# Upper and lower f16 halves of the keys written in place by ScalarE and VectorE, and value loads of two batches called earlier

## The chip, the cores and the metric

The kernel runs on one core of a Trainium2 chip. A core has five engines that run side by side, each in its own order: TensorE (PE, matrix products), VectorE (DVE), ScalarE (ACT), GpSimd (POOL) and SyncE (SP, which here only issues DMAs). 16 DMA engines move data between HBM and the on-chip memory SBUF, which has 128 partitions. The metric is the device time of one execution in microseconds (us).

## The reference

Three layers follow one another: attention over 4 batches, 8 heads, 576 positions and 64 dimensions; a layer of eight experts with one expert for each of 2304 tokens; a layer with squared rectification.

```python
scores = scale * np.matmul(q, k.transpose(0, 1, 3, 2))
psi_rel = np.log1p(np.abs(pos[:, None] - pos[None, :]))
x = (psi_rel / psi_i)[..., None]
bias = np.maximum(x @ w1 + b1, 0.0) @ w2
scores = scores + bias.transpose(2, 0, 1)[None]
attn = softmax(scores)
x = np.matmul(attn, v)                       # tokens x 512
expert_idx = np.argmax(xn @ en.T / tau, axis=1)
out[mask] = gate_w[mask, None] * (np.maximum(x[mask] @ w1[e], 0) @ w2[e])
r = np.maximum(out @ w_in, 0.0)
return (r * r) @ w_out
```

The change lies in the attention only: in how the keys k are brought into the form in which the score products read them.

## The kernel before, in words

Attention fills the time to about 390 us, the experts run to about 640 us, the last layer to the end. The attention works on 72 units (128 positions of one batch and one pair of heads), each in two half steps, one for each head. In a half step (the loop over `hs` in `attention`) every engine gets a fixed set of instructions in a fixed order: TensorE computes scores (`emit_qk`, L498), transposes the exponentials of an earlier half step (`emit_T`, L531) and multiplies with the values (`emit_pv`, L556); VectorE adds the position bias and takes the extreme (`emit_max`, L509); ScalarE takes the exponential (`emit_exp`, L522); one of the two copies the transposed values (L207 on ScalarE, L209 on VectorE). The schedule is written by hand. Twelve half steps with negative numbers come first, in which `first(i)` computes the first bias groups.

Beside the units run background tasks, each a generator that does one piece at a time and then gives way (`yield E_`). `bg(hs, f, ...)` starts one at a half step, `at(hs, f, ...)` calls a function once. `room` lets a task wait while the load counted for ScalarE ("A") or VectorE ("D") is above a limit, until a due half step; `take` and `give` count buffers. Engine queues run in order: an instruction that waits holds everything emitted behind it on its engine, and a DMA that waits for its data holds SyncE's queue.

The scores need f16 precision twice over: a key is split in an upper half (f16 of 8k) and a lower half (8k minus the upper, in f16). The tile `kst[b]` has 128 partitions: for the first head of a pair the upper half lies in partitions 0 to 63 and the lower half in 64 to 127, for the second head the other way round, so that one product of 128 rows sums both. `kst[0]` holds batches 0 and 1, `kst[2]` batches 2 and 3, with four head pairs (`pr`) in each.

Before, each of the eight (batch pair, head pair) blocks is loaded (`k_load`, L227) into a `wr` buffer of 128 partitions with two batches of 576 keys. `k_hi` (L232) writes the upper half of all 128 partitions with one ScalarE instruction into a `wh` buffer, `k_lo` (L237) the lower half with one VectorE instruction, and `k_move` (L246, L247) brings them with four DMAs of 64 partitions each to their rows of `kst`. For batches 0 and 1 `first` does this (`FK` names the steps), for batches 2 and 3 the task `prep_k`, started at half steps 6 to 9. There are two `wr` and two `wh` buffers. The task `presplit` (32 times from half step 14, one each 2.6 half steps) uses the same buffers for the second expert weights: load (L465), three steps of wait, product on GpSimd (L471), two steps, difference on VectorE (L475), store (L479). The values of batches 1, 2, 3 are loaded (`load_v`, L307) at half steps 0, 16 and 20.

Of the kernel before, what the change touches and what calls it, by code (L numbers as in the profile page):

```python
# [8 lines left out]
F16 = mybir.dt.float16  # L9
U32 = mybir.dt.uint32  # L10
I32 = mybir.dt.int32
AF = mybir.ActivationFunctionType
ALU = mybir.AluOpType
# [4 lines left out]
B, H, S, D = 4, 8, 576, 64  # L18
# [5 lines left out]
P = 128  # L24
# [11 lines left out]
QS, KS = -2.0, 8.0  # L36
# [47 lines left out]
def body(ctx: ExitStack, tc: tile.TileContext, q, k, v, wsm, emb, tau, mw1, mw2, win, wout, cst_d, lsk_d, ids_d, out):  # L84
    nc = tc.nc
    win, wout = win.bitcast(U32), wout.bitcast(U32)
    PE, ACT, DVE, POOL, SP = nc.tensor, nc.scalar, nc.vector, nc.gpsimd, nc.sync
# [39 lines left out]
    def attention(actx, bctx, cctx, smp, mid, early, G):  # L127
# [10 lines left out]
        whp = bp("a_wh", 2)  # L138
# [45 lines left out]
        def take(r, n=1):  # L184
            while free[r] < n:
                yield E_
            free[r] -= n

        def later():
            if now[0] > 8:  # L190
                yield E_

        def give(r, n=1):
            free[r] += n

        def room(e, n, due=1000):
            while load[e] > 0 and load[e] + n > LIM and now[0] < due:
                yield E_
# [12 lines left out]
        def A(n, extra=0.09):  # L211
            load["A"] += n * 0.000833 + extra

        def V(n, extra=0.07):
            load["D"] += n * 0.00104 + extra
# [11 lines left out]
            SP.dma_start(out=t, in_=k[b:b + 2, pr].rearrange("b p s -> p b s"))  # L227
            return t

        def k_hi(t):  # L230
            kh = whp.tile([P, 2, 2, S], F16, name="wh")
            ACT.activation(kh[:, 0], t, AF.Copy, scale=KS)  # L232
            A(2 * S)
            return kh

        def k_lo(t, kh):
            DVE.scalar_tensor_tensor(out=kh[:, 1], in0=t, scalar=KS, in1=kh[:, 0], op0=ALU.mult, op1=ALU.subtract)  # L237
            V(2 * S)

        def k_move(b, pr, kh, eng=SP):  # L240
            if b not in kst:
                kst[b] = (G["kv"].rearrange("p (r h b s) -> p r h b s", r=NP, h=2, b=2) if b == 0 else
                          kvp.tile([P, NP, 2, 2, S], F16, name="kst", bufs=1))
            for h2 in range(2):
                r, o = slice(64 * h2, 64 * h2 + 64), slice(64 - 64 * h2, 128 - 64 * h2)
                eng.dma_start(out=kst[b][r, pr, h2], in_=kh[r, 0])  # L246
                eng.dma_start(out=kst[b][o, pr, h2], in_=kh[r, 1])  # L247
            kready.add((b, pr))

        def prep_k(b, pr, wait):  # L250
            due = 8 * b + 4 * pr
            yield from take("wr")
            t = k_load(b, pr)
            for _ in range(wait):
                yield E_
            yield from take("wh")
            yield from room("A", 1.1, due - 8)
            kh = k_hi(t)
            yield E_
            yield from room("D", 1.3, due - 7)  # L260
            k_lo(t, kh)
            give("wr")
            yield from later()
            k_move(b, pr, kh)
            give("wh")


        def q_load(c, b):
# [79 lines left out]
        def first(i):  # L348
# [41 lines left out]
            for j in range(4):  # L390
                x = "k%d" % j
                if i == FK[j]:
                    f_in[x] = f_in[x], k_hi(f_in[x])
                if i == FK[j] + 1:
                    k_lo(*f_in[x])
                    if j < 2:
                        f_in["k%d" % (j + 2)] = k_load(0, j + 2)
                    else:
                        give("wr")
                if i == FK[j] + 2:  # L400
                    k_move(0, j, f_in[x][1])
                    if j > 1:
                        give("wh")

        for r in ("wr", "wh", "qraw"):
            free[r] = 0
        FQ = 1, 8
        FK = 2, 5, 9, 9
# [51 lines left out]
        def presplit(i):  # L460
            e, j = divmod(i, 4)
            s = W2S
            yield from take("wr")
            wr = wrp.tile([P, 2, S], F32, name="wr").rearrange("p b s -> p (b s)")[:, :1024]
            SP.dma_start(out=wr, in_=mw2[e, j])  # L465
            for _ in range(3):
                yield E_
            yield from take("wh")
            wf = whp.tile([P, 2, 2, S], F16, name="wh").rearrange("p a b s -> p (a b s)")[:, :2048]
            wh = wf.rearrange("p (a n) -> p a n", a=2)  # L470
            POOL.tensor_tensor(out=wh[:, 0], in0=wr, in1=w2s_c.to_broadcast([P, 1024]), op=ALU.mult)  # L471
            for _ in range(2):
                yield E_
            yield from room("D", 1.2)
            DVE.scalar_tensor_tensor(out=wh[:, 1], in0=wr, scalar=s, in1=wh[:, 0], op0=ALU.mult, op1=ALU.subtract)  # L475
            V(1024)
            yield E_
            give("wr")
            SP.dma_start(out=wsc2[i * P:(i + 1) * P, :], in_=wf)  # L479
            yield E_  # L480
            yield E_
            give("wh")
# [287 lines left out]
        def at(hs, f, *a):  # L770
            side.setdefault(max(HS0, hs), []).append((f, a, None))
# [9 lines left out]
        for pr in range(NP):  # L781
            bg(int(6 + 1 * pr), prep_k, 2, pr, 3)
        for b in range(1, 4):
            at((HS0 + 2, HS0 + 12, 16, 20)[b], load_v, b)
        at(26, lambda: SP.dma_start(out=id_d.rearrange("(p n) c -> p (n c)", p=P), in_=ids_d.bitcast(U32)))
        bg(-4, consts)
        bl = list(bfirst)
# [797 lines left out]
```

## Time and profile before

| what | us |
|---|---|
| three runs | 1024.21, 1023.83, 1018.97 |
| their median | 1023.83 |
| profiled execution, its own time | 1020.09 |
| its span in the profile | 1018.3 |
| TensorE busy in the span | 946.7 (93%) |
| VectorE busy | 662.0 (65%) |
| ScalarE busy | 540.9 (53%) |
| GpSimd busy | 499.1 (49%) |

TensorE's granted clock over the span is 0.978 of full speed. A busy share is a mean over stages with different limits, and TensorE's matmuls overlap in the pipeline, so 93% does not mean that it works at its peak. The profile names for each instruction the idle time before it and what ended it; these waits are what tells a transfer that holds an engine from one that is hidden.

### The profile page before, as it was taken

How to read it: one execution, taken by the hardware profiler on the slowest of the kernel's cores; microseconds unless marked ns; L12 is line 12 of the kernel's file. 1: busy time of each engine (PE TensorE's matmuls, PEld its weight loads, DVE VectorE, ACT ScalarE, POOL GpSimd, SP SyncE). 2: the span in 40 equal slices, each digit the busy share in tenths (PEclk: the TensorE clock that was granted, in tenths of full speed). 3: DMA queues.
4: the chain of work that ended last, by engine and by line, in shares of the span. 5: the costliest groups of instructions: out<-in, count | busy, mean ns of one | idle time of the engine just before them, and what ended most of it. 6: DMA issues, size and time to landing. Idle time of an engine off the chain costs nothing. (4 is left out here: it accounts for less than half of the span.)

```text
span 1018.3 us, 24810 instructions
## 1 busy us (share of the span) xinstructions
PE 946.7 (93%) x9725; PEld 747.8 (73%) x9725; DVE 662.0 (65%) x1229; ACT 540.9 (53%) x1000; POOL 499.1 (49%) x415
## 2 busy tenths in 40 slices
PE   8687988999899889999999899999999999999995
PEld 4355766677577767776666667688888888888884
DVE  6655899888997874677776767245446455545441
ACT  5666776767777683467565555255423333233330
POOL 1212536446534353366548797275454554645631
PEclk9789999999999999999999999999999999999998
DMA  9998885898779434599899484462011111111000
GB/s 296 318 254 264 305 279 179 267 268 286 226 234 330 163 126 176 213 338 334 325 361 340 146 291 151 153 258 53 22 54 43 32 52 43 32 53 22 22 12 32
DMA packets 78843, 187.17 MB, mean 184 GB/s; under 512 B 26648, under 2 KB 26776, under 8 KB 76128
## 3 DMA queue, kind: packets, MB, share of 16 engines
q1 hardware_dynamic: 72656, 169.98, 49.5%
q0 software_dynamic: 6064, 15.54, 4.4%
q8 instruction: 78, 1.28, 0.5%
q14 instruction: 45, 0.37, 0.1%
HBM read 171.65 MB, written 51.73 MB: 219 GB/s over the span
## 5 line engine op out<-in xcount | busy, mean ns | idle before, releaser
L1436 POOL TENSOR_TENSOR gf<-gf 128x256 f32<-128x256 f32 x144 | 166.0, 1172 | 131.0 <-DVE gf L1433 108.8
L1420 PE MATMUL pf<-big,wih 128*128 128x256 f16 x1728 | 196.0, 273 | 1.5 <-PEq L1374 1.5
L1420 PEld LDWEIGHTS <-wih 128*128 128x128 f16 x1728 | 169.0, 98 | 21.6 <-issue 2.0
L1458 PEld LDWEIGHTS <-g 128*128 128x128 f16 x1512 | 147.4, 98 | 18.7 <-issue 1.0
L1426 ACT ACTIVATE gf<-pf 128x512 f32<-128x512 f32 x72 | 42.5, 597 | 193.3 <-PE pf L1420 140.3
L1220 PE MATMUL ph<-x,w1b 128*128 128x128 f16 x2112 | 127.5, 220 | 7.9 <-DVEq L1024 3.0
L1220 PEld LDWEIGHTS <-w1b 128*128 128x128 f16 x2112 | 122.0, 99 | 13.1 <-DVEq L1024 3.5
L471 POOL TENSOR_TENSOR wh<-wr,w2s_c 128x1024 f16<-128x1024 f32 x32 | 62.2, 1943 | 135.9 <-DMA wr<-in_mw_dram 65.0
L1235 PE MATMUL py<-vt,h 128*128 128x512 f16 x528 | 119.4, 383 | 3.8 <-DMA vt<-wsc 3.8
L1444 DVE TENSOR_TENSOR g<-gf,g 128x1792 f16<-128x1792 f32 x36 | 85.5, 2374 | 50.1 <-ACT g L1443 50.1
L522 ACT ACTIVATE pr<-ssb,mn 128x576 f32<-128x576 f32 x144 | 111.7, 776 | 10.3 <-DVE mn L509 10.3
L509 DVE CUSTOM_DVE_ANT_0 ssb<-ps_s,bias 128x576 f32<-128x576 f32 x144 | 107.4, 749 | 3.1 <-DMA bias<-bias_d 2.2
L1433 DVE TENSOR_TENSOR gf<-gf 128x1024 f32<-128x1024 f32 x28 | 34.3, 1226 | 113.6 <-ACT gf L1426 113.6
L498 PE MATMUL ps_s<-kst,qd 128*128 128x288 f16 (+1 forms) x640 | 96.6, 292 | 11.7 <-DVE mn L509 9.2
L1235 PEld LDWEIGHTS <-h 128*128 128x128 f16 x528 | 51.3, 99 | 63.0 <-issue 7.0
L531 PE MATMUL ps_t<-cst,pr 128*128 128x128 f32 x576 | 92.1, 283 | 2.5 <-DVE pl L607 1.3
L531 PEld LDWEIGHTS ps_t<-cst,pr 128*128 128x128 f32 x576 | 64.9, 144 | 25.7 <-issue 20.8
L556 PE MATMUL pv<-pt,vt 128*64 128x128 f32 (+1 forms) x1280 | 83.6, 274 | 0.0
L498 PEld LDWEIGHTS <-qd 128*128 128x128 f16 (+1 forms) x640 | 56.2, 101 | 26.6 <-issue 16.4
L556 PEld LDWEIGHTS pv<-pt,vt 128*64 128x64 f32 x1280 | 65.5, 140 | 12.5 <-issue 11.4
L1226 DVE SCALAR_TENSOR_TENSOR h<-ph,h 128x512 f16<-128x512 f32 x44 | 30.3, 690 | 49.9 <-ACT h L1225 35.0
L1443 ACT CAST g<-gf 128x1792 f16<-128x1792 f32 x36 | 60.3, 1676 | 4.4 <-POOL gf L1436 4.4
(194 smaller groups left out, 1571.9 us busy)
## 6 DMA issues: line engine op xcount, KB each, us to landing
vt<-wsc SPq DMA_DIRECT2D x88, 512.0 KB
wr<-in_mw_dram SPq DMA_DIRECT2D x76, 512.0 KB
kst<-in_mw_dram SPq DMA_DIRECT2D x44, 512.0 KB
wsc<-wh SPq DMA_DIRECT2D x32, 512.0 KB
bias<-bias_d SPq DMA_DIRECT2D x16, 576.0 KB
bias_d<-rt SPq DMA_DIRECT2D x28, 295.5 KB
qd<-qh SPq DMA_DIRECT2D x64, 128.0 KB
wr<-in_win_dram SPq DMA_DIRECT2D x8, 1024.0 KB
```

The source lines that it names most:

```text
L471: POOL.tensor_tensor(out=wh[:, 0], in0=wr, in1=w2s_c.to_broadcast([P, 1024]), op=ALU.mult)
L498: PE.matmul(s[r, hf, :288], lhsT=qd[:, h2, i, pr, r], rhs=kst[x - x % 2][:, pr, h2, x % 2, js], start=(i == 0), stop=(i == 1))
L509: DVE.tensor_tensor_reduce(out=ss.rearrange("p (a j) -> p a j", a=2), in0=s[:, :, :288], in1=btile[bkey[u]][:, h2].rearrange("p (a j) -> p ...
L522: ACT.activation(pr_sb[k_ // 2][:, h2], ssb.pop(k_), AF.Exp, bias=mns.pop(k_), scale=-1.0, accum_out=sums[c, b][:, h:h + 1])
L531: PE.transpose(pt_ps[k_][:, jc * P:(jc + 1) * P], src[:, j0:j0 + P], eye)
L556: PE.matmul(pv[o, cs], lhsT=vb[:, 2 * jc + h2, d] if jc < 4 else vb[o, 8, d], rhs=a[h2][:, jc, cs] if jc < 4 else e[o, cs], start=(jc == 4 ...
L1220: PE.matmul(p_[:, f4, :], lhsT=w[:, a, kc, f * P:(f + 1) * P], rhs=x2[:, b, kc, :], start=(i == 0), stop=(i == 11))
L1235: PE.matmul(p_, lhsT=h2[:, a, fc, :], rhs=wb2[fc // 2][:, b, fc % 2, :], start=(i == 0), stop=(i == 23))
L1420: PE.matmul(p_[:, h], lhsT=wih[:, a, kc, f * P:(f + 1) * P], rhs=y2[:, b, kc, :], start=(i == 0), stop=(i == 11))
L1436: POOL.tensor_tensor(out=g[:, d], in0=g[:, x], in1=g[:, y], op=op)
L1444: DVE.tensor_tensor(out=gt[:, 1, :, c:c + 2, :], in0=g[:, 1:8], in1=gt[:, 0, :, c:c + 2, :], op=ALU.subtract)
L1458: PE.matmul(ps, lhsT=gt[:, a, s, c, :], rhs=woh[:, c, b, w, :], start=(i == 0 and first), stop=(i == 23 and end), skip_group_check=True)
```

## The change

The upper half is written by ScalarE straight into `kst`, in two instructions of 64 partitions, one for each head of the pair. The lower half is written by VectorE straight into the other 64 partitions of `kst`, again in two instructions; they read the upper half from `kst`. `k_move` and its 32 DMAs go, and the keys no longer use a `wh` buffer. `presplit`, the other user of these buffers, waits two steps instead of three between its load and GpSimd's product, and has both `wh` buffers from the start. The values of batches 2 and 3 are loaded at half steps 14 and 17 instead of 16 and 20.

```diff
-        def k_hi(t):
-            kh = whp.tile([P, 2, 2, S], F16, name="wh")
-            ACT.activation(kh[:, 0], t, AF.Copy, scale=KS)
-            A(2 * S)
-            return kh
-        def k_lo(t, kh):
-            DVE.scalar_tensor_tensor(out=kh[:, 1], in0=t, scalar=KS, in1=kh[:, 0], op0=ALU.mult, op1=ALU.subtract)
-            V(2 * S)
-        def k_move(b, pr, kh, eng=SP):
+        def k_hi(b, pr, t, h2):
             if b not in kst:
                 kst[b] = (G["kv"].rearrange("p (r h b s) -> p r h b s", r=NP, h=2, b=2) if b == 0 else
                           kvp.tile([P, NP, 2, 2, S], F16, name="kst", bufs=1))
-            for h2 in range(2):
-                r, o = slice(64 * h2, 64 * h2 + 64), slice(64 - 64 * h2, 128 - 64 * h2)
-                eng.dma_start(out=kst[b][r, pr, h2], in_=kh[r, 0])
-                eng.dma_start(out=kst[b][o, pr, h2], in_=kh[r, 1])
-            kready.add((b, pr))
+            r = slice(64 * h2, 64 * h2 + 64)
+            ACT.activation(kst[b][r, pr, h2], t[r], AF.Copy, scale=KS)
+            A(2 * S)
+        def k_lo(b, pr, t, h2):
+            r, o = slice(64 * h2, 64 * h2 + 64), slice(64 - 64 * h2, 128 - 64 * h2)
+            DVE.scalar_tensor_tensor(out=kst[b][o, pr, h2], in0=t[r], scalar=KS, in1=kst[b][r, pr, h2],
+                                     op0=ALU.mult, op1=ALU.subtract)
+            V(2 * S)
+            if h2:
+                kready.add((b, pr))
...
-            yield from take("wh")
-            yield from room("A", 1.1, due - 8)
-            kh = k_hi(t)
-            yield E_
-            yield from room("D", 1.3, due - 7)
-            k_lo(t, kh)
+            for h2 in range(2):
+                yield from room("A", 1.1, due - 8)
+                k_hi(b, pr, t, h2)
+            yield E_
+            for h2 in range(2):
+                yield from room("D", 1.3, due - 7)
+                k_lo(b, pr, t, h2)
             give("wr")
-            yield from later()
-            k_move(b, pr, kh)
-            give("wh")
...
                 if i == FK[j]:
-                    f_in[x] = f_in[x], k_hi(f_in[x])
+                    for h2 in range(2):
+                        k_hi(0, j, f_in[x], h2)
                 if i == FK[j] + 1:
-                    k_lo(*f_in[x])
+                    for h2 in range(2):
+                        k_lo(0, j, f_in[x], h2)
...
-                if i == FK[j] + 2:
-                    k_move(0, j, f_in[x][1])
-                    if j > 1:
-                        give("wh")
-        for r in ("wr", "wh", "qraw"):
+        for r in ("wr", "qraw"):
             free[r] = 0
...
-            for _ in range(3):
+            for _ in range(2):
                 yield E_
             yield from take("wh")
...
-            at((HS0 + 2, HS0 + 12, 16, 20)[b], load_v, b)
+            at((HS0 + 2, HS0 + 12, 14, 17)[b], load_v, b)
```

## Rows read from the trace of the kernel before

**Rows 1.** Stretches: length, busy time by engine (instructions), granted clock, DMA share, GB/s

```profile
core 0: us, PE busy (x) PEld busy (x) DVE busy (x) ACT busy (x) POOL busy (x), PEclk, DMA share, GB/s
48.00:50.00 2.00, 2.00 (x23) 1.71 (x19) 1.74 (x5) 1.76 (x6) 0.00 (x0) 1.00 1.05 395
54.00:70.00 16.00, 13.48 (x132) 9.05 (x132) 13.68 (x32) 13.68 (x33) 1.92 (x2) 0.99 0.84 195
64.00:66.00 2.00, 2.00 (x26) 1.41 (x24) 1.86 (x5) 0.51 (x1) 0.00 (x0) 1.00 1.05 205
...
72.00:74.00 2.00, 2.00 (x17) 1.26 (x16) 0.00 (x0) 0.00 (x0) 0.00 (x0) 0.50 1.07 268
...
76.00:92.00 16.00, 15.52 (x156) 12.34 (x152) 12.79 (x35) 13.03 (x32) 1.90 (x1) 0.98 0.84 240
100.00:340.00 240.00, 224.99 (x2509) 165.88 (x2507) 212.51 (x529) 173.67 (x445) 112.26 (x63) 0.99 0.80 260
```

**Rows 2.** TensorE in order of time: start, duration, instruction, idle time before and releaser

```profile
42.79 0.66 PE L531 MATMUL ps_t<-cst,pr 128*128 128x128 f32 x4
...
68.54 0.33 PE L536 MATMUL pv<-cst,pr 128*128 128x128 f32 x1 [1.66 <-ACT big L207]
68.71 0.60 PE L531 MATMUL ps_t<-cst,pr 128*128 128x128 f32 x4
71.36 1.12 PE L498 MATMUL ps_s<-kst,qd 128*128 128x288 f16 x4 [2.06 <-DMA kst<-wh]
...
76.22 0.77 PE L531 MATMUL ps_t<-cst,pr 128*128 128x128 f32 x4
...
91.14 0.60 PE L531 MATMUL ps_t<-cst,pr 128*128 128x128 f32 x4
...
98.67 0.69 PE L556 MATMUL pv<-pte,vt 64*64 64x128 f32 x4 [6.43 <-DMA vt<-in_v_dram]
...
101.19 1.12 PE L531 MATMUL ps_t<-cst,pr 128*128 128x128 f32 x4
```

**Rows 3.** Instructions on buffer wh: count, duration in ns (min/median/max), first and last start

```profile
L475 DVE SCALAR_TENSOR_TENSOR wh<-wr,wh x32: 1209/1222/2862, 92.2 to 332.9; 128x1024 f16<-128x1024 f32 x32
...
L246 SPq DMA_DIRECT2D kst<-wh x16: 462/570/1133, 16.8 to 87.5; - x16
L247 SPq DMA_DIRECT2D kst<-wh x16: 461/600/1632, 17.4 to 88.1; - x16
L232 ACT ACTIVATE wh<-wr x8: 1152/1162/1187, 10.4 to 80.3; 128x1152 f16<-128x1152 f32 x8
L237 DVE SCALAR_TENSOR_TENSOR wh<-wr,wh x8: 1346/1356/1360, 13.4 to 82.9; 128x1152 f16<-128x1152 f32 x8
```

**Rows 4.** VectorE in order of time, same columns as TensorE's

```profile
32.42 1.36 DVE L237 SCALAR_TENSOR_TENSOR wh<-wr,wh 128x1152 f16<-128x1152 f32 x1 [1.75 <-ACT wh L232]
...
37.56 0.76 DVE L509 CUSTOM_DVE_ANT_0 ssb<-ps_s,bias 128x576 f32<-128x576 f32 x1 [2.24 <-DMA bias<-bias_d]
...
60.94 1.35 DVE L237 SCALAR_TENSOR_TENSOR wh<-wr,wh 128x1152 f16<-128x1152 f32 x1
62.22 0.74 DVE L509 CUSTOM_DVE_ANT_0 ssb<-ps_s,bias 128x576 f32<-128x576 f32 x1
```

**Rows 5.** ScalarE in order of time

```profile
65.49 1.17 ACT L232 ACTIVATE wh<-wr 128x1152 f16<-128x1152 f32 x1 [1.85 <-DMA wr<-in_k_dram]
```

**Rows 6.** SyncE in order of time

```profile
81.47 0.47 SPq L246 DMA_DIRECT2D kst<-wh  x1
...
88.13 0.59 SPq L247 DMA_DIRECT2D kst<-wh  x1
...
89.40 0.61 SPq L307 DMA_DIRECT2D vt<-in_v_dram  x1
```

**Rows 7.** GpSimd's L471 and VectorE's L475 in time; then L471's waits (us, times)

```profile
123.01 1.90 POOL L471 TENSOR_TENSOR wh<-wr,w2s_c 128x1024 f16<-128x1024 f32 x1 [4.09 <-DMA wr<-in_mw_dram]
126.11 2.45 DVE L475 SCALAR_TENSOR_TENSOR wh<-wr,wh 128x1024 f16<-128x1024 f32 x1
...
317.62 1.90 POOL L471 TENSOR_TENSOR wh<-wr,w2s_c 128x1024 f16<-128x1024 f32 x1 [2.17 <-DMA wr<-in_mw_dram]
320.61 1.22 DVE L475 SCALAR_TENSOR_TENSOR wh<-wr,wh 128x1024 f16<-128x1024 f32 x1
...
  DMA wr<-in_mw_dram: 65.0, 20
...
  DVE wh L475: 4.7, 2
```

## The prediction, before the change was run

> **What bounds the kernel now.** I read four views in this order. First the stretches by 2 us, to see where TensorE stands still while the DMA engines do not: from 48 to 50 us the DMA share is 1.05 at 395 GB/s and TensorE works, from 64 to 66 the share is the same but only 205 GB/s go through, and from 72 to 74 TensorE runs at a granted clock of 0.50, its 1.2 GHz level, while VectorE and ScalarE do nothing [rows 1]. Then TensorE in order of time. The transposes of L531 come once per half step and serve as its clock: from 42.79 to 68.71 lie 12 steps (2.16 us each), from 76.22 to 91.14 seven (2.13). Between these two runs stands one step of 7.51 us, in which a matmul of the scores waits until 71.36 for a key move, and behind them one of 10.05 us, in which the product with the values waits 6.43 us, until 98.67, for a load of values [rows 2]. So in the first 100 us the end is set twice by a transfer and not by an engine. Third the instructions on the keys' buffer (durations and counts) [rows 3], fourth VectorE, ScalarE and SyncE around the edits [rows 4 to 6]. Behind 100 us VectorE is busy 212.51 of 240 us (89%) and TensorE 225 [rows 1]: there a saving on transfers is worth nothing, but work or waits put on VectorE cost. The half steps are emitted in a fixed order that no measured time changes, so a stall that goes is not made up by later work being called earlier; what is behind 400 us should only shift.
>
> **The change part by part.** All sums are against the profiled execution, 1020.09 us (span 1018.3 and 1.8 around it).
>
> *The moves.* 32 SyncE moves of 144 KB go. Eight of them carry 1.18 MB, which at 395 to 205 GB/s [rows 1] is 3.0 to 5.8 us of all DMA engines; each also held SyncE's queue for about 0.57 us [rows 3]. **Stall one**: nothing can wait for a move any more, and what the matmul at 71.36 needs is then VectorE's lower half, which is written four steps ahead. VectorE and ScalarE were idle here, so nothing else is late next: 7.51 - 2.15 = **-5.4** (the half-clock matmuls up to 76.22 are inside this number). It could be -4.4 if the next value load or a bias read is a microsecond late.
>
> *Values at 14 and 17.* The fourth value load is issued at 89.40, 9.3 us ahead of its use [rows 2, 6]. Three half steps earlier is 6.5 us; the eight moves issued from 81 to 88 us also leave the queue, 3.0 us at least. Together 9.5, more than the wait of 6.43. **Stall two**: 10.05 - 2.15 = **-7.9**, with the half clock behind it included. Against it: the issue stands in SyncE's order behind the first load of the second expert weights, which must wait until a key buffer is free, and the third value load and these weights fill the queue at the same time. If only half comes, -3.9; if the load comes no sooner than the queue empties, -3.
>
> *Two instructions in place of one, start.* An instruction's time goes with its elements in one partition, so half the partitions is no saving: each key pair costs one more lower half on VectorE, 1.28 us from start to next start [rows 4] (1.356 long), and one more upper half on ScalarE, 1.16 [rows 3]. For batches 0 and 1 that is 4 x 1.28 = 5.1 us on VectorE before the first scores are taken up at 37.56. What is queued behind them on VectorE are the bias rectifications, the bias evictions and that first score instruction; TensorE's first transposes wait for all of these. Out of this chain go VectorE's wait of 1.75 us for an upper half that itself waited for a buffer that a move held, and the last wait of 2.24 us for the bias read [rows 4], which had eight moves ahead of it. 5.1 - 4.0 = 1.1; ScalarE's 4 x 1.16 stands ahead of evictions that VectorE's second parts follow, and I put 0.6 for this: **+1.7**. Bounds: -2.2 (all extra work in idle places, the bias read 2.24 sooner) to +4.1 (ScalarE adds 3.0).
>
> *The same for batches 2 and 3.* Again 4 x 1.28 = 5.1 us on VectorE and 4.6 on ScalarE, between 54 and 92 us. VectorE is idle 2.3 us from 54 to 70 and 3.2 from 76 to 92, ScalarE 2.3 and 3.0 [rows 1]. The cover is as large as the work, but blocks of two instructions stand ahead of a score instruction and an exponential: I let half hide, **+2.6**, bounds 0 and +5.1. In front of one upper half ScalarE waits 1.85 us for a key load [rows 5], and TensorE 1.66 us for ScalarE behind it [rows 2]; with fewer moves in the queue I take half of that off, **-0.8** (0 to -1.7).
>
> A start partition other than the output's is new on VectorE. The Trainium skill (VectorE: DVE Perf Modes, section "Two Vector instructions with no wait between them") says in my words that an instruction is held until the earlier ones are finished when the quadrant of an input or of the output differs from the one last used. The lower halves now start 0.07 us before the one ahead has ended [rows 4]; by this rule the 16 of them and the 8 or so behind would lose that, an estimate of 24 x 0.07 = 1.7 us on VectorE, and no row here shows a case of it. The sum would be a microsecond worse.
>
> *The split of the second expert weights.* Its buffer is no longer shared with keys, and one step of wait goes between its load and GpSimd's product. GpSimd's product waits for the load in 20 of 32 cases, 65.0 us in all [rows 7], so the product starts no sooner; VectorE's difference is emitted one step (2.3 us) sooner and stands in VectorE's order with score instructions behind it. VectorE waited for GpSimd twice only, 4.7 us in all. But of the 32 pairs eight between 123 and 321 us have less than 2.3 us between GpSimd's end and VectorE's start, the first 1.2 and the last 1.1 us [rows 7]; one step less leaves VectorE waiting there for the missing part, 10.8 us in all. VectorE's 11% idle time and the two score buffers hide some, and a longer step widens the gaps again: **+3**, bounds -2 (the splits end some ten steps earlier) and +10.8. The differences also lengthen beside GpSimd's products, 2862 ns at most against a median of 1222 [rows 3], and the last lower halves of the keys may now meet these: inside the bound. The Trainium skill (SBUF — State Buffer, section "SBUF: two separate sides") calls this an exclusive lock on a port that VectorE instructions with two inputs share with GpSimd; the row agrees.
>
> **Sum**: 1.7 + 2.6 - 0.8 - 5.4 - 7.9 + 3 = -6.8, so 1013.3 on the profile's scale. The profile lies 3.7 us under the median of the three runs (1023.83) and 1.1 over the fastest; a median of the changed kernel may lie on either side of its own profile, and I add half of the 3.7, 1.9, to each case: **1015 us**. On this scale the kernel before stands at 1022.
>
> **The rivals.**
> 1. *The engines hide nothing.* Start +4.1, later keys +5.1, key load 0, stalls -13.3, splits +3: -1.1, **1021**. For it: VectorE is busy 13.68 of 16 us from 54 to 70 [rows 1]. Against it: the stalls themselves leave VectorE idle 7 us and more.
> 2. *The value load does not really come sooner* (the change doesn't do what it says): half of stall two stays, +4 on the sum: **1019**. For it: DMA share 1.05 just before [rows 1]; against it: the moves that made up much of that are gone.
> 3. *Slower: VectorE waits for GpSimd in each split.* Place: the differences of L475 behind 100 us; price: 10.8 us in full, because VectorE is 89% busy there; it decides from the point at which a load takes more than the remaining steps. With nothing hidden on the keys: -13.3 + 4.1 + 5.1 + 10.8 = +6.7, **1029**.
> 4. *More than forecast*: keys hidden and splits free: 1.7 - 0.8 - 13.3 = -12.4, **1010**.
>
> **How the numbers follow.** Forecast 0.45, more than forecast 0.16, engines hide nothing 0.17, value load late 0.10, slower 0.12. A change of under 0.5% (5.1 us) is about what a measurement of this kernel can't tell from none. Forecast and rival 4 are faster by more: 0.61. Rivals 1 and 2 are within: 0.27. Rival 3: 0.12. The range leaves out the ends of rivals 3 and 4: 1005 to 1027; the forecast's own is 1011 to 1018.
>
> **What would show it.** Right: no step over 4 us between 42 and 110 us in TensorE's order; no wait for keys or values; VectorE's first score instruction at 38 to 40 us; granted clock 1.00 from 45 us on. Stall two wrong: a wait of L556 for a value load. Start wrong: the first score instruction under 36 or over 42 us. Split wrong: waits of L475 for GpSimd that sum to under 2 or over 12 us. The prediction fails as a whole if the steps behind 110 us are on average not the same as before to 0.05 us.

## The result, and the profile after

The changed kernel is slower: 1029.23 us (median of 8, 1026.62 to 1034.25) against 1018.82 for the kernel before (8 runs, 1015.85 to 1024.66, the three listed ahead among them). The ratio is 1.0088 with a 95% interval of 1.0065 to 1.0111, about 9 us. Its profiled execution took 1030.99 us with a span of 1029.2, against 1020.09 and 1018.3 before; the prediction was 1015, on a scale with the kernel before at 1022. Executions of one program differ by about 1%, and the profiled one of e6_moves_wait3 below was a slow one, so only its ratio and its start are read.

TensorE in order of time (start, duration, instruction, idle time before it and its releaser) shows what became of the two stalls:

```profile
47.91 0.66 PE L523 MATMUL ps_t<-cst,pr 128*128 128x128 f32 x4
...
70.91 0.65 PE L490 MATMUL ps_s<-kst,qd 128*128 128x288 f16 x4 [1.98 <-DVE mn L501]
...
73.88 1.12 PE L523 MATMUL ps_t<-cst,pr 128*128 128x128 f32 x4
76.36 0.60 PE L523 MATMUL ps_t<-cst,pr 128*128 128x128 f32 x4
78.59 1.12 PE L490 MATMUL ps_s<-kst,qd 128*128 128x288 f16 x4 [1.64 <-DVE mn L501]
82.77 0.66 PE L523 MATMUL ps_t<-cst,pr 128*128 128x128 f32 x4
...
88.65 0.33 PE L528 MATMUL pv<-cst,pr 128*128 128x128 f32 x1 [1.04 <-ACT big L207]
```

No matmul waits for a key or for values any more; the wait of 6.43 us that stood at 98.67 [rows 2] is gone. But where the key move had been waited for, TensorE now waits for VectorE (1.98 and 1.64 us), and the step from 76.36 to 82.77 is 6.41 us long. VectorE and ScalarE at this place, same columns:

```profile
67.32 2.74 DVE L240 SCALAR_TENSOR_TENSOR kst<-wr,kst 64x1152 f16<-64x1152 f32 x2
70.09 0.76 DVE L501 CUSTOM_DVE_ANT_0 ssb<-ps_s,bias 128x576 f32<-128x576 f32 x1
...
73.85 0.47 DVE L329 TENSOR_SCALAR rt<-ps_b,cst 128x240 f32<-128x240 f32 x1 [2.69 <-ACT rt L327]
...
75.02 2.72 DVE L240 SCALAR_TENSOR_TENSOR kst<-wr,kst 64x1152 f16<-64x1152 f32 x2
77.77 0.76 DVE L501 CUSTOM_DVE_ANT_0 ssb<-ps_s,bias 128x576 f32<-128x576 f32 x1
```

```profile
70.90 2.34 ACT L235 ACTIVATE kst<-wr 64x1152 f16<-64x1152 f32 x2 [2.27 <-DMA wr<-in_k_dram]
73.26 0.55 ACT L327 ACTIVATE rt<-ps_b,cst 128x352 f32<-128x352 f32 x1
73.72 0.76 ACT L514 ACTIVATE pr<-ssb,mn 128x576 f32<-128x576 f32 x1
```

Two lower halves stand as a block of 2.7 us right in front of a score instruction of VectorE, and that is what TensorE waits for. ScalarE waits 2.27 us for a key load (1.85 before [rows 5]) and then spends 2.34 us on a pair, in front of a bias eviction for which VectorE waits 2.69 us. TensorE's granted clock shows it too (0.50 is its 1.2 GHz level):

```profile
core 0: us, PE busy (x) PEld busy (x) DVE busy (x) ACT busy (x) POOL busy (x), PEclk, DMA share, GB/s
10.00:20.00 10.00, 5.64 (x43) 2.35 (x47) 8.62 (x18) 6.11 (x9) 2.32 (x4) 0.85 0.83 278
20.00:30.00 10.00, 7.55 (x50) 2.96 (x43) 6.63 (x13) 6.39 (x9) 0.00 (x0) 0.81 0.46 142
...
72.00:74.00 2.00, 2.00 (x19) 1.67 (x18) 0.15 (x1) 1.96 (x4) 0.00 (x0) 0.50 0.97 272
...
100.00:340.00 240.00, 221.43 (x2422) 161.47 (x2423) 205.71 (x510) 171.79 (x435) 117.89 (x65) 0.98 0.82 262
```

From 72 to 74 us the clock is at 0.50 as before [rows 1], now with ScalarE busy 1.96 of the 2 us. In the same 240 us from 100 to 340 VectorE finishes 510 instructions where it finished 529, and TensorE 2422 where it had 2509 [rows 1]. Two losses thus lie outside the two stalls: at the start, and behind 110 us.

**The start.** VectorE, then ScalarE, then (last fence) VectorE before the change, from its second profiled execution (below):

```profile
14.28 0.27 DVE L329 TENSOR_SCALAR big<-ps_s,cst 128x48 f32<-128x48 f32 x1 [1.26 <-ACT big L327]
...
21.32 0.30 DVE L329 TENSOR_SCALAR pr<-ps_s,cst 128x80 f32<-128x80 f32 x1 [1.38 <-ACT pr L327]
...
24.82 0.32 DVE L329 TENSOR_SCALAR big<-ps_s,cst 128x96 f32<-128x96 f32 x1 [1.34 <-ACT big L327]
25.15 2.72 DVE L240 SCALAR_TENSOR_TENSOR kst<-wr,kst 64x1152 f16<-64x1152 f32 x2
...
35.73 5.45 DVE L240 SCALAR_TENSOR_TENSOR kst<-wr,kst 64x1152 f16<-64x1152 f32 x4 [0.36 <-ACT kst L235]
...
42.40 0.76 DVE L501 CUSTOM_DVE_ANT_0 ssb<-ps_s,bias 128x576 f32<-128x576 f32 x1 [0.60 <-DMA bias<-bias_d]
```

```profile
10.56 2.33 ACT L235 ACTIVATE kst<-wr 64x1152 f16<-64x1152 f32 x2
...
20.59 0.69 ACT L327 ACTIVATE pr<-ps_s,cst 128x512 f32<-128x512 f32 x1 [4.42 <-PE ps_s L360]
...
34.54 4.71 ACT L235 ACTIVATE kst<-wr 64x1152 f16<-64x1152 f32 x4
```

```profile
20.36 1.35 DVE L237 SCALAR_TENSOR_TENSOR wh<-wr,wh 128x1152 f16<-128x1152 f32 x1
...
39.16 0.76 DVE L509 CUSTOM_DVE_ANT_0 ssb<-ps_s,bias 128x576 f32<-128x576 f32 x1 [3.81 <-DMA bias<-bias_d]
```

The second key pair comes 4.79 us later on VectorE (25.15 against 20.36): one more lower half, and waits of 1.26, 1.38 and 1.34 us for evictions of ScalarE, where there had been 0.34, 0.51 and none. The first and the third of these evictions stand behind two upper halves on ScalarE. The second does not: ScalarE itself waits 4.42 us there for TensorE (20.59), and TensorE had waited 3.14 us for a rectification of VectorE, behind the first pair's lower halves. Part of the loss comes back at the end, where the wait for the bias read shrinks to 0.60 us, from 3.81 in this profile of before and 2.24 in the first [rows 4]. TensorE's granted clock is 0.85 and 0.81 in the two stretches shown above.

### The profile page after: what moved, and what is told of

Same layout as the page of the kernel before. It is cut to its first block, busy times and chain, and to the rows that moved or that the text cites. A ratio compares the mean times of both kernels' runs of the same rounds, so it can differ in the third digit from the quotient of the medians.

```text
span 1029.2 us, 24768 instructions
## 1 busy us (share of the span) xinstructions
PE 954.1 (93%) x9725; PEld 751.4 (73%) x9725; DVE 668.8 (65%) x1236; ACT 552.7 (54%) x1009; POOL 501.6 (49%) x415
## 3 DMA queue, kind: packets, MB, share of 16 engines
q8 instruction: 78, 1.28, 0.5%
## 5 line engine op out<-in xcount | busy, mean ns | idle before, releaser
L463 POOL TENSOR_TENSOR wh<-wr,w2s_c 128x1024 f16<-128x1024 f32 x32 | 64.6, 2020 | 136.2 <-DMA wr<-in_mw_dram 105.7
L207 ACT COPY pt<-ps_t 128x512 f32<-128x512 f32 x101 | 58.1, 575 | 8.8 <-PE ps_t L523 8.7
```

## The experiments

VectorE's score instruction runs once per half step, 144 times (numbers 0 to 143), and cuts each profile at the same places of the program. The table has the start of number 0 and the length of three stretches from such starts, all in us; 8 to 28 holds the two stalls of before. "Behind 143" is the time from the start of number 143 to the end of the span: the end of the attention, the experts and the last layer. "Hold" is for how many half steps at least a split's load holds one of its two `wr` buffers (waits ahead of GpSimd's product, between it and VectorE's difference, and behind that). Ratios are to the kernel before on the same chip, with 95% intervals. The runs come from several chips: e1 to e4 from one on which the kernel before took 1021.41 us, e5 to e7 and before_again from one with 1019.84, e8 to e11 from one with 1028.65. No profile of before was taken on this last chip, so stretches in us are best compared within a chip.

| kernel | hold | number 0 | 8 to 28 | 28 to 104 | 104 to 143 | behind 143 | ratio |
|---|---|---|---|---|---|---|---|
| before | 6 | 37.56 | 56.1 | 185.3 | 83.8 | 639.7 | 1 |
| before_again | 6 | 39.16 | 54.3 | 183.4 | 85.1 | 639.0 | |
| the change | 5 | 42.40 | 52.6 | 191.0 | 88.0 | 639.2 | 1.0088 (1.0065 to 1.0111) |
| e1_values_only | 6 | 40.53 | 55.1 | 178.9 | 86.9 | 643.0 | 0.9960 (0.9923 to 0.9997) |
| e2_after_wait3 | 6 | 44.25 | 53.4 | 177.4 | 88.0 | 647.5 | 1.0041 (1.0014 to 1.0068) |
| e3_start_moves | 5 | 37.45 | 50.0 | 189.4 | 87.4 | 640.0 | 1.0028 (0.9993 to 1.0063) |
| e4_later_moves | 5 | 41.16 | 58.6 | 195.4 | 85.5 | 638.6 | 1.0174 (1.0104 to 1.0245) |
| e5_doubled | 6 | 43.29 | 55.6 | 180.0 | 85.3 | 642.9 | 1.0089 (1.0054 to 1.0125) |
| e6_moves_wait3 | 6 | 38.50 | | | | | 0.9986 (0.9951 to 1.0021) |
| e7_values_wait2 | 5 | 37.99 | 56.5 | 191.1 | 82.1 | 641.2 | 1.0090 (1.0059 to 1.0121) |
| e8_wait2_spaced | 6 | 38.95 | 55.8 | 185.3 | 88.2 | 640.9 | 0.9992 (0.9967 to 1.0017) |
| e9_wait2_then3 | 6 | 36.91 | 52.6 | 185.4 | 90.4 | 642.6 | 1.0026 (0.9992 to 1.0060) |
| e10_values_wait4 | 7 | 36.53 | 52.4 | 180.7 | 90.4 | 652.5 | 1.0006 (0.9985 to 1.0027) |
| e11_values_3then3 | 7 | 36.76 | 54.4 | 179.9 | 93.7 | 651.3 | 1.0055 (1.0031 to 1.0079) |

### One part alone: the values

```diff
-            at((HS0 + 2, HS0 + 12, 16, 20)[b], load_v, b)
+            at((HS0 + 2, HS0 + 12, 14, 17)[b], load_v, b)
```

> The kernel before with one edit of the change: values of batches 2 and 3 loaded at half steps 14 and 17. Engines theory (the change lost because each key half costs a second instruction, and the earlier values are its only gain): the wait of 6.43 us for values goes, the key moves stay, 6 to 9 us under the kernel before. Transfer theory (the queue is the limit, whatever is called first): the wait moves to another load, within 3 us of before.

Measured 0.996: the earlier values are worth 4 us (0.3 to 7.9 by the interval), half of what was put for stall two and between the two forecasts. VectorE's rows of this run where stall two had been, and one of TensorE's:

```profile
98.75 1.23 DVE L475 SCALAR_TENSOR_TENSOR wh<-wr,wh 128x1024 f16<-128x1024 f32 x1 [3.18 <-POOL wh L471]
...
103.98 1.23 DVE L475 SCALAR_TENSOR_TENSOR wh<-wr,wh 128x1024 f16<-128x1024 f32 x1 [2.73 <-POOL wh L471]
```

```profile
105.94 0.65 PE L498 MATMUL ps_s<-kst,qd 128*128 128x288 f16 x4 [2.60 <-DVE mn L509]
```

TensorE no longer waits for the values, but VectorE comes to the first differences of the split sooner than GpSimd's products are there, waits 3.18 and 2.73 us in front of score instructions, and TensorE waits 2.60 us for it. The stall had hidden this. Stall one is still there, with a wait of 2.77 us for a key move at 74.62, and the stretch 8 to 28 is hardly shorter (55.1 against 56.1 and 54.3), so the 4 us rest on the ratio.

### One part undone: the wait, the start, the later keys

Three kernels, each the changed kernel with one part as before. e2_after_wait3:

```diff
-            for _ in range(2):
+            for _ in range(3):
                 yield E_
             yield from take("wh")
```

> The changed kernel with one edit undone: three steps of wait in the split of the second expert weights, not two. Splits theory (the 10 us that the changed kernel loses between half steps 68 and 104 come from that step): 8 to 10 us under the changed kernel, about 1019. Engines theory: within 3 us of the changed kernel, about 1029.

e3_start_moves (batches 0 and 1 by moves; in e4_later_moves the same in `prep_k`, for batches 2 and 3):

```diff
-                    for h2 in range(2):
-                        k_hi(0, j, f_in[x], h2)
+                    f_in[x] = f_in[x], m_hi(f_in[x])
...
-                    for h2 in range(2):
-                        k_lo(0, j, f_in[x], h2)
+                    m_lo(*f_in[x])
...
+                if i == FK[j] + 2:
+                    k_move(0, j, f_in[x][1])
...
```

> The changed kernel with the keys of batches 0 and 1 prepared as before, one instruction for each half and DMA moves; those of batches 2 and 3 written in place. Engines theory: the first score instruction is back at 37.6 us (it stood at 42.4), so 5 us under the changed kernel or a little less where moves crowd the queue, about 1024 to 1026. Splits theory: the same 5 us, and the loss between half steps 68 and 104 stays.

> The changed kernel with the keys of batches 2 and 3 prepared as before, one instruction for each half and DMA moves; those of batches 0 and 1 written in place. Engines theory: steps 11 to 23 lose 5 us of VectorE's work and the matmul of half step 15 waits for a move again (5 us), the two about equal: within 3 us of the changed kernel. Transfer theory: slower than the changed kernel by 5 us or more.

Against the 1.0088 of the change, the step of wait costs 4.8 us (to 1.0041), the start in place 6.1 us (to 1.0028), and the keys of batches 2 and 3 in place gain 8.8 us here (to 1.0174, from four runs only, so anything from about 1 to 16). The 4.8 us lie between what the two theories said for e2; e3 came out as forecast; for e4 the transfer theory was right and the engines theory was not. VectorE's differences of the split in the changed kernel and in e2_after_wait3 (count, duration in ns as min/median/max, first and last start):

```profile
L467 DVE SCALAR_TENSOR_TENSOR wh<-wr,wh x32: 1206/1219/2443, 116.1 to 336.6; 128x1024 f16<-128x1024 f32 x32
```

```profile
L467 DVE SCALAR_TENSOR_TENSOR wh<-wr,wh x32: 1214/1219/2687, 118.7 to 358.5; 128x1024 f16<-128x1024 f32 x32
```

With one step less the 32 splits begin within 3 us of the same time and end 22 us sooner: they are packed more closely into the stretch where VectorE is full. From number 28 to 143 the change takes 13.5 us longer than e2 (279.0 against 265.4), but behind 143 it takes 8.3 us less (639.2 against 647.5): in e2, where the splits run until 358.5, TensorE's first matmul of the expert blocks comes 12.5 us after the start of number 143, in the change and before 8.2 us.

### Two parts undone, and the step of wait by itself

e6_moves_wait3 is e3_start_moves with the three steps of e2_after_wait3. e7_values_wait2 is e1_values_only with two steps.

> The changed kernel with two of its parts undone: the keys of batches 0 and 1 go through moves again, and the split of the second expert weights has its three steps of wait; the keys of batches 2 and 3 stay in place and the values at 14 and 17. Theory engines and splits together: the start costs 6 us (the run with start moves alone stood at 1.0028, the change at 1.0088) and the shorter wait 5 us (1.0041 against 1.0088), and both add up, so 1.0088 - 0.0060 - 0.0047 = 0.998, about 1019 us beside 1021. The first score instruction starts near 38 us, the splits run from about 109 to 350 us and the stretch from step 28 to step 104 is as long as with three steps of wait before (177 to 185 us). Rival, both are the same loss (what comes late in the start pushes the splits into the full stretch, and either cure takes it away): 1.003 as with either alone.

> The kernel before with the values of batches 2 and 3 at half steps 14 and 17 and with two steps of wait in the split in place of three; all keys stay with their moves and their buffers. It differs from the run with the earlier values alone (0.996) in that one step. Theory splits: the step by itself costs 5 us, whatever happens to the keys, so 0.996 + 0.005 = 1.001; more splits fall between steps 28 and 104 (25 or 26 in place of 23) and that stretch is 5 us longer or more. Rival, the step costs only where the key buffers come free late: 0.996 again. Rival, direct waits: VectorE's idle time for GpSimd in the split grows by 5 us or more against the run with the earlier values alone.

e6 gives 0.9986: the two costs add up, as the first theory said (0.998). So the start in place costs 5.6 us with three steps (1.0041 - 0.9986) and 6.1 with two. Against e1 (0.996) no gain of the keys of batches 2 and 3 in place is seen with three steps: 2.7 us the wrong way, with intervals that overlap. e7 gives 1.0090: on the kernel with moves the step costs 13.3 us, more than the theory said. Against e7, e3 (1.0028) has these keys in place with two steps, and gains 6.3 us. The idle time of VectorE's difference that ended with GpSimd's product (us in all, times, longest), in e7 and then in e1:

```profile
DVE wh L475 <- POOL wh L471: 19.2, 8, 7.9
```

```profile
DVE wh L475 <- POOL wh L471: 9.0, 4, 3.2
```

Two things are thus seen at once: 10 us more direct waits, and a stretch from 28 to 104 that is 12 us longer, with 26 splits in it in place of 23 (the one behind it is 4.8 us shorter, 82.1 against 86.9). The longest of these waits, with GpSimd's product in front of it and TensorE's wait behind it, all in e7:

```profile
94.30 1.89 POOL L471 TENSOR_TENSOR wh<-wr,w2s_c 128x1024 f16<-128x1024 f32 x1 [32.18 <-DMA kst<-wh]
```

```profile
96.23 1.22 DVE L475 SCALAR_TENSOR_TENSOR wh<-wr,wh 128x1024 f16<-128x1024 f32 x1 [7.93 <-POOL wh L471]
```

```profile
99.55 1.12 PE L498 MATMUL ps_s<-kst,qd 128*128 128x288 f16 x4 [6.83 <-DMA kst<-wh]
```

The first product of the splits waits until a key move has left the shared buffer. With two steps the difference is called so soon behind it that VectorE stands for 7.93 us, and TensorE for 6.83; the profile puts these down to a key move, but VectorE's score instruction behind the difference ends only at 99.50 as well. In e4_later_moves VectorE waits 7.04 us at the same place and TensorE 5.93; in e3 and in the change, where these keys do not use the buffer, the first difference does not wait. The stretch 8 to 28 shows it: 50.0 in e3 against 56.5 in e7, 52.6 in the change against 58.6 in e4. So writing these keys in place is worth about 6 us there with two steps, with stall one in it. With three steps this stretch was not read in such a pair.

### The second instructions alone

```diff
-            ACT.activation(kh[:, 0], t, AF.Copy, scale=KS)
-            A(2 * S)
+            for r in (slice(0, 64), slice(64, 128)):
+                ACT.activation(kh[r, 0], t[r], AF.Copy, scale=KS)
+                A(2 * S)
...
-            DVE.scalar_tensor_tensor(out=kh[:, 1], in0=t, scalar=KS, in1=kh[:, 0], op0=ALU.mult, op1=ALU.subtract)
-            V(2 * S)
+            for r in (slice(0, 64), slice(64, 128)):
+                DVE.scalar_tensor_tensor(out=kh[r, 1], in0=t[r], scalar=KS, in1=kh[r, 0], op0=ALU.mult, op1=ALU.subtract)
+                V(2 * S)
```

> The kernel before with each half of a key pair written in two instructions over 64 partitions in place of one over 128, into the same buffer as before and moved from there by the same 32 moves; values and splits as before. It puts the price of the second instructions on VectorE and ScalarE alone, without the shift of partitions and without any saving of moves. Theory engines: the start becomes 4 to 6 us longer (first score instruction at 41 to 43 us in place of 37.6), batches 2 and 3 add 2 to 5 us, in all 1.006 to 1.010. Rival, the cost lies in writing to rows of other partitions than those read (each instruction held until the one ahead is done) or in the order of the reads: start longer by under 2 us, 1.000 to 1.004.

Measured 1.0089, 9 us (5.5 to 12.8): the second instructions alone cost as much as the whole change, with the buffer, the moves, the values and the split of the kernel before. Its start is that of the change (43.29 against 42.40). The rest of the 9 us is not located: number 143 starts 2.6 to 2.8 us later than in the two profiles of before, 3.2 to 3.9 us more come behind it, with splits that run until 360.8, and this profiled execution lay 5 us under the median of the run. And TensorE's waits in this kernel from 40 to 116 us are these (the first belongs to the start):

```profile
PE ps_e L756 <- issue: 8.2, 1, 8.2
PE ps_s L500 <- DVE mn L511: 7.1, 5, 1.9
PE pv L538 <- ACT big L207: 1.9, 3, 1.0
PE ps_t L533 <- ACT pt L207: 0.9, 1, 0.9
```

All 32 moves and the late value loads are still there, and TensorE, VectorE and ScalarE wait for none of them in this stretch: the engines have become so late that the transfers are in time. Only GpSimd still waits for moves, in front of its first two products, and no difference of VectorE waits there for it. What removing the moves gives on top was not measured by itself. e2_after_wait3, with the values early and the moves gone, stands at 1.0041, 4.9 us under e5, good to some 4 us. If the earlier values were worth their 4.1 us here too, e5 would come to 1.0049 and the moves would be worth nothing; but nothing waits for values in e5, and if the earlier calls are worth nothing here, the moves are worth the 4.9 us. No run decides between the two.

### Pace or direct wait

Both from e7_values_wait2; e8_wait2_spaced keeps the buffers one step longer, e9_wait2_then3 puts the step between product and difference:

```diff
             V(1024)
             yield E_
+            yield E_
             give("wr")
```

```diff
             POOL.tensor_tensor(out=wh[:, 0], in0=wr, in1=w2s_c.to_broadcast([P, 1024]), op=ALU.mult)
-            for _ in range(2):
+            for _ in range(3):
                 yield E_
```

> The kernel before with the earlier values and two steps of wait in the split, as the run that stood at 1.009, and one more half step after VectorE's difference before its two buffers are given back. GpSimd's product still comes two steps behind its load and the difference two steps behind that, but a buffer is held as long as with three steps, so the splits follow one another at the old pace. Theory density (packing more splits into the stretch where VectorE is full is what costs): back near the 0.996 of three steps, 22 or 23 splits between steps 28 and 104, that stretch 179 to 183 us. Rival, direct waits (the load is not there after two steps, GpSimd's product is late and VectorE stands in front of its difference): 1.006 to 1.010, VectorE's idle time for GpSimd's product stays at 15 us or more.

> The kernel before with the earlier values, two steps of wait between the split's load and GpSimd's product and three, not two, between the product and VectorE's difference: the difference stands where it stood before the change, the buffers are held as long as before, and only GpSimd's product is one step sooner in its order. Theory density and theory direct waits both expect about 0.996 here, with VectorE's idle time for GpSimd's product at 9 us or less. Rival, GpSimd's own order (its product waits for the load in front of bias rectifications and routing work that others need): 1.004 or more.

e8 gives 0.9992 and e9 1.0026, so of the 13 us a buffer held one step longer gives back 10 and 6.5. The waits of VectorE's difference in e8, GpSimd's first product there, and the waits in e9:

```profile
DVE wh L475 <- POOL wh L471: 10.6, 8, 2.4
DVE wh L475 <- DMA kst<-wh: 6.9, 1, 6.9
```

```profile
94.91 1.90 POOL L471 TENSOR_TENSOR wh<-wr,w2s_c 128x1024 f16<-128x1024 f32 x1 [31.75 <-DMA kst<-wh]
```

```profile
DVE wh L475 <- POOL wh L471: 8.9, 5, 2.8
```

The 6.9 us stand in front of the first difference, at 96.84, 0.03 us after GpSimd's product has ended (94.91 + 1.90): it is the wait of 7.93 us of e7, put down to the move that GpSimd had waited for. In all e8 waits 17.5 us against 19.2 in e7, and is 10 us faster by the ratio; e9 waits 8.9 us, and is no faster than e8. So the direct waits do not set the time here. The direct waits theory had the waits of e8 right and its time wrong; the density theory came near on the time and had 23 splits between 28 and 104, but missed the length of that stretch (185.3 against 179 to 183). e9 came out as neither theory said. What is left between e8, e9 and the 0.996 of e1 (3 to 7 us, the 3 within the noise) stays open, and so does the choice between their two places for the step.

The table shows the pace: 28 to 104 takes 189.4 and 195.4 us with a hold of 5 and 178.9 and 177.4 with 6 (e1 to e4), 191.1 and 180.0 to 183.4 (e5, e7 and before_again), 191.0 and 185.3 (the change and before, whose chips are not on record).

### A still slower pace

e10_values_wait4 has four steps in place of e1's three ahead of the product; e11_values_3then3 has three and then three in place of two.

> The kernel before with the earlier values and four steps of wait in the split in place of three. Theory density: fewer splits fall into the stretch from step 28 to 104 (about 20), which becomes up to 5 us shorter, and the rest falls into the slack behind it: 0.990 to 0.995. Theory direct waits: VectorE's idle time for GpSimd's product (9.0 us with three steps) falls to 3 us or less, 0.990 to 0.995 as well. Rival, the loss with two steps is a threshold that three steps already clear: 0.996, or above it if the splits that come later lengthen the end of the attention.

> The kernel before with the earlier values, three steps of wait between the split's load and GpSimd's product as before, and three in place of two between the product and VectorE's difference. A buffer is held as long as with four steps of wait. Theory density: the same as with four steps, 0.990 to 0.995. Theory direct waits: the same too if it is VectorE's wait for a late product (9.0 us falls to 3 or less). Rival, GpSimd's own wait for its load in front of other work is what a longer first wait would cure: 0.996 here, and less only with four steps.

1.0006 and 1.0055: no gain, so the forecast of the density theory fails for the whole time. For the stretch it holds on the chip of e8 to e11: 19 splits from 28 to 104 and 180.7 and 179.9 us, against 185.3 and 185.4 in e8 and e9 with a hold of 6. But the splits end so late that the expert blocks wait, and behind number 143 come 652.5 and 651.3 us where e8 and e9 have 640.9 and 642.6; this is the rival named for e10. VectorE's differences in e10, and TensorE's first instructions of the expert blocks from 384 us on (count, then busy time and mean, then idle time ahead):

```profile
L475 DVE SCALAR_TENSOR_TENSOR wh<-wr,wh x32: 1214/1220/2544, 94.2 to 370.2; 128x1024 f16<-128x1024 f32 x32
```

```profile
L1203 PE MATMUL px<-eye,xs 128*128 128x128 f16 x32 | 2.9, 232 | 5.7 <-ACT xs L1036 2.9 <-POOL xs L1038 2.8
```

In e1 the last difference starts at 329.4 and the same line waits 0.0 us. So the pace has a good value between two losses, one inside the full stretch and one behind it, and three steps are near it.

### The kernel before once more

> The kernel before once more, unchanged, for a second profile of it: how far the start, the steps around the two stalls and the stretch behind 110 us differ between two executions of one program. If the steps of a profile repeat, the first score instruction starts within 1 us of 37.56 and the stretch from step 28 to step 104 within 2 us of 185.3; if a single profile does not carry differences of 3 us, one of these lies further off.

1019.51 us, span 1017.7. Two profiles of one program differ by 1.6 us at the start, by 1.8 in the stretch 8 to 28 and by 1.9 in 28 to 104 (table). The first lies outside the 1 us that was expected. Over the ten kernels whose start was not touched number 0 begins anywhere from 36.5 to 40.5 us, over the four with doubled instructions there from 41.2 to 44.3, on average 4.7 us later. So a difference of 2 us between single profiles carries nothing here, and at the start not one of 4 us.

## Why the prediction was wrong

With ratios times 1020 us, a path of runs from before to the change has four terms that can be set beside the parts of the sum. Two orders are on record, one by e1, e6 and e2, one by e1, e7 and e3:

| part | predicted | measured | by | other order | by |
|---|---|---|---|---|---|
| values, stall two | -7.9 | -4.1 | e1 against before | -4.1 | e1 against before |
| batches 2 and 3 in place: stall one -5.4, instructions +2.6, key load -0.8 | -3.6 | +2.7 | e6 against e1 | -6.3 | e3 against e7 |
| batches 0 and 1 in place | +1.7 | +5.6 | e2 against e6 | +6.1 | the change against e3 |
| split | +3 | +4.8 | the change against e2 | +13.3 | e7 against e1 |
| sum | -6.8 | +9.0 | | +9.0 | |

Each term is good to some 4 to 5 us, and the sums agree because either path ends at the change. The later keys and the split depend on each other: together they were put at -0.6 and cost 7 to 7.5 us in both orders. Read by place in the profiles, the two of before first:

| stretch | predicted | before (two) | the change | difference |
|---|---|---|---|---|
| start of number 0 | +1.7 | 37.56, 39.16 | 42.40 | +3.2 to +4.8 |
| 8 to 28: both stalls and the later keys | -11.5 | 56.1, 54.3 | 52.6 | -1.8 to -3.6 |
| 28 to 143: the split | +3 | 269.1, 268.4 | 279.0 | +9.9 to +10.5 |
| behind 143 | 0 | 639.7, 639.0 | 639.2 | about 0 |

- **Stall one** and with it the stretch 8 to 28 failed most, at the words "VectorE and ScalarE were idle here, so nothing else is late next". They were idle because the stall held them. With the move gone VectorE's next work is late: two lower halves stand in front of a score instruction, TensorE waits 1.98 and 1.64 us for it, and the step from 76.36 to 82.77 takes 6.41 us. With the start left as before (e3) the stretch comes to 50.0, still some 6 us short of the gain that was put. The sign was that no step over 4 us would be left. When the second instructions were added with the moves kept (e5), the waits for the moves went by themselves. The cover for these instructions (+2.6) was read from stretches that leave out 70 to 76 us, so the two terms do not use the same idle time; the chances do, where the idle time of the stalls speaks against the first rival.
- **Stall two** was right in its mechanism (no wait for values after) and mis-sized: -4.1. The step that failed is 10.05 - 2.15, which lets everything behind the stall run at the usual step. In e1 the next thing late is GpSimd's product, 3.18 and 2.73 us. In time the load did not come sooner: in the changed kernel it is issued at 89.56 as against 89.40 [rows 6], three half steps sooner by number, and the steps themselves are later.
- **The start** came out above its upper bound of 4.1, at 5.6 to 6.1 by the ratios and 4.7 on average by the profiles. The 0.6 us put for ScalarE was the term: VectorE waits 4.0 us for ScalarE's evictions (1.26, 1.38 and 1.34), against 0.85 before, partly behind upper halves and partly round by TensorE, which waits for VectorE. That the bias read would come out of the chain was right (0.60 us left), and not enough. The first score instruction at 42.40 is outside the 36 to 42 given as the sign.
- **The key load**: predicted to shorten, it stays (2.27 us after, 1.85 before).
- **The split**: +4.8 lies near the +3 and within its bounds, and by the prediction's sign (waits between 2 and 12 us) it holds too: 7.6 us are put down to GpSimd, 9.9 with one that is put down to a query move, against 4.7 before [rows 7] and 3.4 in e2. What the term left out is the pace. The closer splits lengthen 28 to 143 by 13.5 us against e2, and their earlier end, named as a gain ("bounds -2"), gives back 8.3 behind it. On the kernel with moves the step costs 13.3 us, beyond the upper bound of 10.8.
- **The held instructions.** The four lower halves at 35.73 take 5.45 us, so (5.45 - 1.35) / 3 = 1.37 us from start to start, where 1.28 was read before [rows 4]; in e5_doubled, without the shift of partitions, four take 5.51. The rule of the Trainium skill named in the prediction (VectorE: DVE Perf Modes, section "Two Vector instructions with no wait between them") has an instruction at another start quadrant held until the earlier ones have finished; the trace agrees. At about 0.09 us for each of 16 this is a microsecond or two, not the cause.
- **The rivals.** The slower one gave 1029 us, which is the measured time, but in part by luck: its scale has the kernel before at 1022, where 1018.82 was measured, and it takes off both stalls in full. Its "nothing hidden on the keys" is what happened, and more; its waits for GpSimd are 7.6 us against 4.7 before, not 10.8 more. Its chance of 0.12 was too low. VectorE's share (13.68 us of 16 busy from 54 to 70 [rows 1]) spoke for the loss and was outvoted, in the first rival, by idle time inside the stalls.
- **Behind 110 us** the steps should have stayed the same to 0.05 us. From score instruction 28 to 143 they take 278.96 us against 269.06, that is 0.086 us more for each of 115. By its own test the prediction fails here.

A version better than both is the kernel before with the earlier values alone: 0.996, 4 us, with an interval that just excludes no change.

## What to carry to other kernels

Idle time inside a stall says nothing of what comes when it is gone: take the stall out first, find what is late next, and only then ask what the new work costs. Replacing a DMA by two half-width instructions on engines that are over 85% busy there can cost more than the DMA, since an instruction over 64 partitions takes as long as one over 128 (medians of 1353 against 1356 ns on VectorE, 1161 against 1162 on ScalarE). Background work that fills a full stretch has a pace with a loss on both sides, so a wait that looks too long should be costed by what it packs together and not only by what it delays.

## What had not been expected of the hardware

- ScalarE gets nothing back from half the partitions either, and its instructions at changing start partitions do not overlap: four upper halves of 64 partitions take 4.71 us, (4.71 - 1.16) / 3 = 1.18 us each, while with 128 partitions the next instruction, of another kind, followed 1.05 us behind such a start (10.53 to 11.58 us in the second profile of before).
- TensorE's granted clock in the start fell from 1.00 to 0.85 and 0.81 (10 to 20 and 20 to 30 us) once it had to wait for VectorE's rectifications, 3.14 us in front of the matmuls at 17.94; 16 of these then took 4.27 us where 16 had taken 3.07. In the profiles of before, with waits of 1.34 us and less between these matmuls, the clock stayed at 1.00 up to 30 us. A delay of engines was thus made longer by TensorE.
